# Holding one GpSimd cast behind a VectorE chain, and emitting half of an S1 sum two units sooner

## The chip, the cores and the metric

The kernel runs on one core of a Trainium2 chip. The metric is device time in microseconds (us); each time below is a median of several executions, but for two runs of one execution each. Positions such as "at 67.10" are us from the start of a profiled span. The span is about 1.8 us shorter than the measured time. The experiments were made in two sessions on two chips, and each is compared with the kernel before of its own session: 263.33 us for e2, e3, e5 and e6, 263.17 us for e7, e8, e10 and e11.

## The reference, cut to what matters

```python
q_s = softmax(q, over d);  k_s = softmax(k, over s)         # 8 batches, 8 heads, 576 x 64
kv  = einsum('bhsd,bhse->bhde', k_s, v)
x   = einsum('bhsd,bhde->bhse', q_s, kv)  -> reshaped to 4608 x 512
h   = x @ w_in                             # 512 -> 2048
out = (h * sigmoid(h)) @ w_out             # 2048 -> 512, float32
```

## The kernel before

The 4608 tokens go in nine chunks of 512. Apart from the start (chunk 0 and half of the first product of chunk 1), both matrix products of a chunk are done with seven block products in place of eight. This needs sums and differences of blocks, which VectorE makes: `S1` to `S4` for the second product. TensorE's program is a list of units of work; `plan(u, f)` emits `f` just ahead of unit `u`. An "h add" is VectorE adding a product, from the PSUM banks where matmuls write, to a sum `h`; it frees these banks for later matmuls. Each engine runs what was emitted for it in order and waits on semaphores where data demand it.

```python
def s_op(t, i, f0=0, f1=HF):                     # on VectorE, both inputs in SBUF
    in0, in1, op = {
        1: (blk(t, 0, 1), blk(t, 1, 1), ALU.add),
        2: (SS[1], blk(t, 0, 0), ALU.subtract),
        3: (blk(t, 0, 0), blk(t, 0, 1), ALU.subtract),
        4: (blk(t, 1, 0), SS[2], ALU.subtract),
    }[i]
    ...
def full(t):                                      # chunks 2 to 6
    ...
    for i, x in ((1, 4), (2, 5), (3, 15), (4, 19)):
        plan(u + x, lambda i=i: s_op(t - 1, i))
    for i in range(2):                            # the attention of the next batch, b = t + 1
        plan(u + (3, 10)[i], lambda i=i: exp_q(b, i))              # ScalarE
        plan(u + (7, 11)[i], lambda i=i: qsum(b, i))               # VectorE: zq, then rzq = 1/zq
        plan(u + (16, 17)[i], lambda i=i: qnorm(b, i, nc.gpsimd))  # GpSimd: eq * rzq
        plan(u + (2, 11)[i], lambda i=i: vcast(b, i, nc.gpsimd))   # GpSimd: v to bf16
    ...
last = NCH - 1
plan(begin[NCH] - 9, lambda: s_op(last, 1, 4, 8))  # half of the last chunk's S1
```

The softmax here doesn't subtract the row's maximum and nothing guards it: scores larger than these inputs give would overflow.

Of the kernel before, what the change touches and what calls it, by code (L numbers as in the profile page):

```python
# [17 lines left out]
def kernel(  # L18
# [9 lines left out]
    nc = tc.nc  # L28
# [12 lines left out]
    NCH = NT // TCH  # L41
# [21 lines left out]
    SS = {i: glob.tile([128, HF, HT], FP16, name=f"S{i}") for i in (1, 2, 4)}  # L63
# [8 lines left out]
    gate = glob.tile([1, 1], FP32, name="gate")  # L72
# [14 lines left out]
    def copy(eng, o, i):  # L87
        if eng is nc.scalar:
            eng.copy(out=o, in_=i)  # L89
        else:  # L90
            eng.tensor_copy(o, i)  # L91

    def load(b, name, src, cc, eng):
        t = ld.tile([128, 2, J * D], FP32, name=name)
        st[b][name, cc] = t
        x = src[b].rearrange("(g r) (p j) d -> g (r p) (j d)", r=2, j=J)
        eng.dma_start(out=t, in_=x.rearrange("g x y -> x g y")[:, 2 * cc:2 * cc + 2, :])

    def jgd(b, name, cc):
        return st[b][name, cc].rearrange("p g (j d) -> p j g d", d=D)  # L100
# [4 lines left out]
    def exp_q(b, cc, g0=0, g1=2):  # L105
        if "eq" not in st[b]:
            st[b]["eq"] = ap.tile([128, J, NG * D], BF16, name="eq")
        nc.scalar.activation(  # L108
            out=half(st[b]["eq"], cc)[:, :, g0:g1], in_=jgd(b, "qt", cc)[:, :, g0:g1], func=ACT.Exp
        )  # L110

    def exp_k(b, cc):
        nc.scalar.activation(out=half(ek, cc), in_=jgd(b, "kt", cc), func=ACT.Exp)  # L113

    def vcast(b, cc, eng, g0=0, g1=2):
        o = vaug[:, :, 2 * cc + g0:2 * cc + g1, 0:D]
        i = jgd(b, "vt", cc)[:, :, g0:g1, :]
        copy(eng, o, i)

    def qsum_pair(b, cc):  # L120
        e = half(st[b]["eq"], cc)
        t1 = mp.tile([128, 2 * TCH], FP32, name="h0", bufs=1)[:, 0:J * D]
        t1 = t1.rearrange("p (j g d) -> p j g d", g=2, d=D // 2)
        t2 = mp.tile([128, 2 * TCH], FP32, name=f"h{cc + 1}", bufs=1)[:, 0:J * D // 2]
        t2 = t2.rearrange("p (j g d) -> p j g d", g=2, d=D // 4)
        nc.gpsimd.tensor_tensor(  # L126
            out=t1, in0=e[:, :, :, 0:D // 2], in1=e[:, :, :, D // 2:D], op=ALU.add
        )
        nc.gpsimd.tensor_tensor(
            out=t2, in0=t1[:, :, :, 0:D // 4], in1=t1[:, :, :, D // 4:D // 2], op=ALU.add  # L130
        )
        st[b]["t2", cc] = t2
# [11 lines left out]
    def qsum(b, cc, gs=None):  # L144
        new_zq(b)
        z, e = st[b]["zq"][:, cc], half(st[b]["eq"], cc)
        if gs is None:
            nc.vector.reduce_sum(out=z, in_=e, axis=AX.X)  # L148
        else:
            nc.vector.reduce_sum(out=z[:, :, gs], in_=e[:, :, gs, :], axis=AX.X)  # L150
        if gs != 0:
            nc.vector.reciprocal(out=st[b]["rzq"][:, cc], in_=z)  # L152

    def qnorm(b, cc, eng):
        e = half(st[b]["eq"], cc)
        r = st[b]["rzq"][:, cc]
        eng.tensor_tensor(  # L157
            out=e, in0=e, in1=r[:, :, :, None].to_broadcast([128, J, 2, D]), op=ALU.mult
        )
# [6 lines left out]
    def q_transpose(b):  # L166
        nc.sync.dma_start_transpose(
            out=new_qt(b).rearrange("x j c y -> x (j c) y"),
            in_=st[b]["eq"].rearrange("x j c -> x (j c)"),
        )  # L170
# [38 lines left out]
    def kv_both(b):  # L209
        kv(b, 0)  # L210
        kv(b, 1)
        kvcopy(b)
# [137 lines left out]
    def group_silu(t, i, f, n):  # L350
        x = group_bank(t, False) if i is None else four(t, i)
        nc.scalar.activation(out=group_out(t, f, n), in_=x, func=ACT.Silu, scale=1.0 / XS)  # L352

    def group(t, g, i, on=None, defer=False):
        bank = 0 if i in (1, 6, 7, 4) else 6 if t == 1 else 2
        w, f0, f1 = WS[g], 4 * g + 8, 4 * g
        a, bb = {
            1: (wa(0, f0), xb(t, 0, 0)),
            2: (wa(1, f0), xb(t, 1, 0)),
            3: (w[3], xb(t, 1, 1)),  # L360
            4: (wa(1, f1), XS4[3]),
            5: (w[0], XS4[0]),
            6: (w[1], XS4[1]),
            7: (w[2], XS4[2]),
        }[i]
        for p in range(4):
            for c in range(2):
                nc.tensor.matmul(  # L368
                    out=PS[:, bank + p // 2, (p % 2) * HT:(p % 2) * HT + width(t)],
                    lhsT=a[:, c, p * 128:(p + 1) * 128],  # L370
                    rhs=bb[:, c, 0:width(t)],
                    start=(i in (1, 2, 5) and c == 0 and p % 2 == 0),
                    stop=(i in (2, 3, 4) and c == 1 and p % 2 == 1),
                    skip_group_check=True,
                )
        on = on or {}
        if i == 1:
            group_snap(t, 0)
        elif i == 2:
            group_add(t, 0)  # L380
        elif i == 6:
            group_snap(t, 1, on.get(1, nc.scalar))
        elif i == 7:
            group_snap(t, 2, on.get(2, nc.scalar))
            group_add(t, 2)
        elif i == 4:
            group_silu(t, None, f1, 0)
        elif i == 3:
            if not defer:
                group_silu(t, 2, f1, 1)  # L390
                group_silu(t, 0, f0, 0)
            group_add(t, 1)
# [37 lines left out]
    def blk(t, kh, th):  # L430
        return GTS[t % 2][:, kh * HF:(kh + 1) * HF, th * HT:(th + 1) * HT]

    def s_op(t, i, f0=0, f1=HF):
# [6 lines that stand above are left out]
        f = slice(f0, f1)  # L440
        o = blk(t, 0, 1) if i == 3 else SS[i]
        nc.vector.tensor_tensor(out=o[:, f], in0=in0[:, f], in1=in1[:, f], op=op)  # L442
# [170 lines left out]
    def plan(u, f):  # L613
        at.setdefault(u, []).append(f)
# [7 lines left out]
    begin = {1: len(units)}  # L622
# [3 lines left out]
    def b_units(t, order):  # L626
        got = []
        for i in order:
            got.append(lambda t=t, i=i: prod(t, i, 0))

            def second(t=t, i=i):
                prod(t, i, 1)
                after(t, i)

            got.append(second)
        return got
# [11 lines left out]
    def full(t):  # L648
        begin[t] = u = len(units)
        b = t + 1  # L650
        bs = b_units(t - 1, ORDER)
        gs = [
            lambda g=g, i=i: group(t, g, i, {1: nc.vector} if g else {2: nc.vector}, True)
            for g in (1, 0)
            for i in ORDER
        ]
        for x in 2 * four_pairs:
            units.append({"b": bs, "g": gs}[x].pop(0))
        for i, x in ((1, 4), (2, 5), (3, 15), (4, 19)):
            plan(u + x, lambda i=i: s_op(t - 1, i))  # L660
        for g, at3 in ((1, (13, 17, 15)), (0, (23, 28, 25))):
            f1, f0 = 4 * g, 4 * g + 8
            for i, x, f, n in zip(range(3), at3, (f0, f0, f1), (0, 1, 1)):
                plan(u + x, lambda i=i, f=f, n=n: group_silu(t, i, f, n))
        more = b + 1 < B
        for i in range(2):
            plan(u + (3, 10)[i], lambda i=i: exp_q(b, i))
            plan(u + (7, 11)[i], lambda i=i: qsum(b, i))
            plan(u + (16, 17)[i], lambda i=i: qnorm(b, i, nc.gpsimd))
            plan(u + (2, 11)[i], lambda i=i: vcast(b, i, nc.gpsimd))  # L670
            plan(u + (6, 4)[i], lambda i=i: exp_k(b, i))
            if more:
                plan(u + (5, 12)[i], lambda i=i: load(b + 1, "qt", q, i, nc.sync))
                plan(u + (8, 6)[i], lambda i=i: load(b + 1, "kt", k, i, nc.sync))
                plan(u + (22, 23)[i], lambda i=i: load(b + 1, "vt", v, i, nc.sync))
        plan(u + 17, lambda: q_transpose(b))
        plan(u + 15, lambda: kv_both(b))
        plan(u + 22, lambda: xt(t + 1, 0, nc.vector))
        plan(u + 27, lambda: xt(t + 1, 1))
        plan(u, lambda: (xs_op(t, 1), xs_op(t, 2), xs_op(t, 3), xs_op(t, 4)))  # L680
# [24 lines left out]

    begin[NCH] = len(units)
    last = NCH - 1
    plan(begin[NCH] - 9, lambda: s_op(last, 1, 4, 8))
    plan(begin[NCH] - 7, lambda: s_op(last, 2, 4, 8))
    plan(begin[NCH], lambda: (s_op(last, 1, 0, 4), s_op(last, 2, 0, 4), s_op(last, 3)))  # L710
    plan(begin[NCH] + 6, lambda: s_op(last, 4))
# [139 lines left out]
```

## Time and profile before

| | before |
|---|---|
| median of 4 executions (of the first 3, which the prediction had: 263.27) | 263.32 us (263.2 to 263.8) |
| span of the profiled one | 261.6 us |
| TensorE busy | 252.6 us, 97% |
| chunk 2: S1 on VectorE | 1.90 us (67.10 to 69.00) |
| chunk 2: second v cast on GpSimd | 66.76 to 67.93 |

In a timeline line the columns are start, duration, engine, source line, operation, output<-input, shapes, and in brackets the idle time before it with what ended it. VectorE is DVE, ScalarE is ACT, GpSimd is POOL, TensorE is PE. To judge a wait of TensorE here, use starts: undisturbed bursts of eight matmuls start 0.87 us apart. What exceeds that is lateness.

This answer for S1's source line, in the kernel before, gives count, shortest, median and longest duration in ns:

```profile
L442 DVE TENSOR_TENSOR S<-GT x9: 681/1215/1897, 67.1 to 245.2; 128x2048 f16<-128x2048 f16 x7, 128x1024 f16<-128x1024 f16 x2
```

The median is 1215 ns and one instance took 1897: the one in chunk 2.

### The profile page before, as it was taken

To read this page: it belongs to the slowest core of one execution; us is meant where nothing else is said; L and a number is where in the kernel's file an instruction comes from. 1 tells how busy PE (TensorE), PEld (TensorE's weight loads), DVE (VectorE), ACT (ScalarE), POOL (GpSimd) and SP (SyncE) were. 2 spreads that over 40 slices of the span, in tenths; PEclk is the share of its full clock that TensorE was granted. 3 is DMA by queue.
4 is the path that set the end of the run, shared out by engine and by line. 5 is a ranking of instruction groups with operands and counts; after the bars stand their busy time and mean duration, and the time that the engine had idled before them with its cause. 6 is when DMAs were issued, how large, how long until landed. Compare 5 with 4: busy or idle time off the path is not lost.

```text
span 261.6 us, 6410 instructions
## 1 busy us (share of the span) xinstructions
PE 252.6 (97%) x2732; PEld 203.2 (78%) x2732; DVE 207.7 (79%) x268; ACT 187.6 (72%) x212; POOL 65.7 (25%) x62
## 2 busy tenths in 40 slices
PE   8799999999999999999999999999999999999992
PEld 3457655656887888888888888888888888888881
DVE  2867797888997999799979997999798548855832
ACT  5766887898994799579957995799573748484610
POOL 1743791651160306030603060306000000000003
PEclk9999999999999999999999999999999999999999
DMA  7999999689979486957794869640534003300624
GB/s 244 335 192 297 299 319 333 259 184 391 307 278 238 111 220 230 205 142 189 262 230 118 218 233 167 180 89 3 90 76 87 3 0 78 85 3 1 139 64 120
DMA packets 35452, 45.89 MB, mean 175 GB/s; under 512 B 16208, under 2 KB 19984, under 8 KB 35424
## 3 DMA queue, kind: packets, MB, share of 16 engines
q1 hardware_dynamic: 29568, 33.69, 47.4%
q0 software_dynamic: 5616, 11.60, 17.0%
q8 instruction: 21, 0.34, 0.5%
q10 hardware_dynamic: 240, 0.20, 0.2%
q14 instruction: 7, 0.06, 0.1%
HBM read 36.70 MB, written 9.44 MB: 176 GB/s over the span
## 4 chain that ended last, share of the span: by engine, by line
PE 79%; DVE 6%; DMA 5%; issue 4%; POOL 3%; ACT 1%; POOLq 0%; DVEq 0%; ACTq 0%
PE PS L468 34%; PE PS L368 33%; PE PS L405 5%; DMA qt<-in_q_dram 5%; PE PS L276 2%; PE PS L228 2%; PE PS L189 2%; DVE h L346 1%; POOL W L545 1%; DVE S L442 1%; DVE GT L442 1%; DVE zq L148 1%; POOL out_dram L730 1%; POOL h L126 0%; DVE h L91 0%
## 5 line engine op out<-in xcount | busy, mean ns | idle before, releaser
L346 DVE TENSOR_TENSOR h<-PS,h 128x1024 f32<-128x1024 f32 (+1 forms) x45 | 54.0, 1199 | 13.0 <-ACT h L89 6.8
L468 PEld LDWEIGHTS <-GT 128*128 128x128 f16 x512 | 49.6, 98 | 6.8 <-issue 1.0
L368 PEld LDWEIGHTS <-WS 128*128 128x128 f16 x480 | 46.8, 98 | 7.2 <-issue 1.1
L468 PE MATMUL PS<-W,GT 128*128 128x256 f16 x384 | 49.1, 273 | 0.0
L368 PE MATMUL PS<-XS,WS 128*128 128x256 f16 (+1 forms) x360 | 46.3, 272 | 0.5 <-DVE h L346 0.5
L352 ACT ACTIVATE GT<-h 128x1024 f16<-128x1024 f32 (+1 forms) x45 | 46.1, 1047 | 0.3 <-DVE h L346 0.3
L89 ACT COPY h<-PS 128x1024 f32<-128x1024 f32 (+1 forms) x35 | 35.1, 1004 | 13.6 <-PE PS L368 13.1
L157 POOL TENSOR_TENSOR eq<-eq,rzq 128x1152 bf16<-128x1152 bf16 x13 | 27.8, 2135 | 58.2 <-DVE rzq L152 56.5
L468 PEld LDWEIGHTS <-S 128*128 128x128 f16 x384 | 37.1, 98 | 5.5 <-issue 1.0
L368 PEld LDWEIGHTS <-W 128*128 128x128 f16 x360 | 34.7, 98 | 4.8 <-issue 0.5
L468 PE MATMUL PS<-T,S 128*128 128x256 f16 x256 | 32.7, 273 | 0.0
L368 PE MATMUL PS<-XT,W 128*128 128x256 f16 (+1 forms) x240 | 29.5, 272 | 0.1
L352 ACT ACTIVATE GT<-PS 128x1024 f16<-128x1024 f32 (+1 forms) x15 | 15.3, 1017 | 18.9 <-PE PS L368 18.9
L91 POOL CAST vaug<-vt 128x1152 bf16<-128x1152 f32 x12 | 14.9, 1242 | 43.7 <-DMA vt<-in_v_dram 34.9
L108 ACT ACTIVATE eq<-qt 128x1152 bf16<-128x1152 f32 (+1 forms) x18 | 19.1, 1059 | 2.7 <-DMA qt<-in_q_dram 2.7
L730 POOL DMA_DIRECT2D out_dram<-ow x5 | 2.7, 546 | 72.5 <-DVE ow L715 72.5
L113 ACT ACTIVATE ek<-kt 128x1152 bf16<-128x1152 f32 x16 | 18.4, 1154 | 1.4 <-DMA kt<-in_k_dram 1.4
L148 DVE TENSOR_REDUCE zq<-eq 128x18 f32<-128x1152 bf16 x12 | 16.1, 1344 | 3.8 <-ACT eq L108 3.8
L258 PE MATMUL PS<-XT,W 128*128 128x288 f16 x128 | 16.6, 286 | 0.5 <-DVE XT L91 0.2
L468 PE MATMUL PS<-W,S 128*128 128x256 f16 x128 | 16.5, 273 | 0.0
L488 DVE SCALAR_TENSOR_TENSOR ow<-PS,sc 128x512 f32<-128x512 f32 x7 | 4.8, 691 | 14.4 <-ACT sc L484 14.4
L258 PEld LDWEIGHTS <-W 128*128 128x128 f16 x128 | 12.3, 97 | 4.9 <-issue 1.6
(78 smaller groups left out, 346.3 us busy)
## 6 DMA issues: line engine op xcount, KB each, us to landing
out_dram<-ow SPq DMA_DIRECT2D x64, 128.0 KB, 2.4
qt<-in_q_dram SPq DMA_DIRECT2D x12, 576.0 KB, 4.6
kt<-in_k_dram SPq DMA_DIRECT2D x12, 576.0 KB, 5.4
vt<-in_v_dram SPq DMA_DIRECT2D x12, 576.0 KB, 5.4
qt<-in_q_dram POOLq DMA_DIRECT2D x4, 576.0 KB, 10.6
kt<-in_k_dram POOLq DMA_DIRECT2D x4, 576.0 KB, 13.3
vt<-in_v_dram POOLq DMA_DIRECT2D x4, 576.0 KB, 12.7
W<-in_moe_w_out_dram POOLq DMA_DIRECT2D x4, 512.0 KB, 14.9
```

The costliest lines, as they stand in the source:

```text
L89: eng.copy(out=o, in_=i)
L91: eng.tensor_copy(o, i)
L108: nc.scalar.activation(out=half(st[b]["eq"], cc)[:, :, g0:g1], in_=jgd(b, "qt", cc)[:, :, g0:g1], func=ACT.Exp)
L113: nc.scalar.activation(out=half(ek, cc), in_=jgd(b, "kt", cc), func=ACT.Exp)
L148: nc.vector.reduce_sum(out=z, in_=e, axis=AX.X)
L157: eng.tensor_tensor(out=e, in0=e, in1=r[:, :, :, None].to_broadcast([128, J, 2, D]), op=ALU.mult)
L258: nc.tensor.matmul(out=PS[:, 2 * (fb % 3) + n, 0:S // 2], lhsT=W1[:, c, fb * 128:(fb + 1) * 128], rhs=XTS[0][:, c, n * (S // 2):(n + 1) * ...
L346: nc.vector.tensor_tensor(out=four(t, i), in0=group_bank(t, True), in1=four(t, i), op=ALU.add)
L352: nc.scalar.activation(out=group_out(t, f, n), in_=x, func=ACT.Silu, scale=1.0 / XS)
L368: nc.tensor.matmul(out=PS[:, bank + p // 2, (p % 2) * HT:(p % 2) * HT + width(t)], lhsT=a[:, c, p * 128:(p + 1) * 128], rhs=bb[:, c, 0:wid ...
L405: nc.tensor.matmul(out=PS[:, 2 + tb, :], lhsT=GTS[t % 2][:, fc, tb * 128:(tb + 1) * 128], rhs=W2[:, fc, :], start=(fc == 0), stop=(fc == N ...
L468: nc.tensor.matmul(out=PS[:, bank, m * HN:(m + 1) * HN], lhsT=a[:, fc, m * 128:(m + 1) * 128], rhs=bb[:, fc, :], start=(first and fc == 0) ...
```

## The change

The intent is to keep the second v cast of chunk 2 off GpSimd until S2 is done, so that it does not run beside S1. A 1x1 copy on GpSimd reads one element of S2, and the cast stands behind it in order. The second part emits half of the last chunk's S1 two units sooner.

```diff
+    def vcast_at(t, b, cc):
+
+        if t == 2 and cc == 1:
+            nc.gpsimd.tensor_copy(gate, SS[2][0:1, 0, 0:1])
+        vcast(b, cc, nc.gpsimd)
...
-            plan(u + (2, 11)[i], lambda i=i: vcast(b, i, nc.gpsimd))
+            plan(u + (2, 6 if t == 2 else 11)[i], lambda i=i: vcast_at(t, b, i))
...
-    plan(begin[NCH] - 9, lambda: s_op(last, 1, 4, 8))
+    plan(begin[NCH] - 11, lambda: s_op(last, 1, 4, 8))
```

## The prediction

> **What bounds the kernel now.** I read three views, from coarse to fine: the page's busy times, the chain of waits cut to chunk 2 (56 to 90 us from the span's start), and the timelines of VectorE, GpSimd and TensorE over the same stretch. The page says who is scarce:
>
> ```profile
> PE 252.6 (97%) x2732; PEld 203.2 (78%) x2732; DVE 207.7 (79%) x268; ACT 187.6 (72%) x212; POOL 65.7 (25%) x62
> ```
>
> TensorE is busy 97% of the span at a granted clock of 0.999. Work taken off another engine buys nothing, unless TensorE stands still waiting for that engine. So the question is only where it stands still. The chain that ended last, in chunk 2, answers it:
>
> ```profile
> 65.05 0.89 PE PS L368 x8
> 65.94 0.02 issue
> 65.96 1.22 DVE h L91
> 67.18 1.82 DVE S L442
> 69.01 0.02 issue
> 69.03 1.23 DVE S L442
> 70.26 1.27 DVE zq L148
> ...
> 75.12 1.08 DVE h L346
> 76.20 2.61 DVE GT L442
> ...
> 79.35 1.23 DVE h L346
> 80.57 0.04 issue
> 80.61 1.03 PE PS L368 x8
> ```
>
> For 14.6 us (65.96 to 80.57) the chain leaves TensorE and lies on VectorE without a break; after 80.61 it is TensorE again until about 253 us, where the closing copies and stores begin. So VectorE sets the end of the kernel only here. Two of its links are long: S1 (1.82 us) and S3 (the GT line, 2.61). The timeline of VectorE, then of GpSimd, shows why:
>
> ```profile
> 67.10 1.90 DVE L442 TENSOR_TENSOR S<-GT 128x2048 f16<-128x2048 f16 x1
> 69.03 1.23 DVE L442 TENSOR_TENSOR S<-S,GT 128x2048 f16<-128x2048 f16 x1
> 76.11 2.70 DVE L442 TENSOR_TENSOR GT<-GT 128x2048 f16<-128x2048 f16 x1
> ```
>
> ```profile
> 66.76 1.16 POOL L91 CAST vaug<-vt 128x1152 bf16<-128x1152 f32 x1 [1.29 <-DMA vt<-in_v_dram]
> 72.03 2.12 POOL L157 TENSOR_TENSOR eq<-eq,rzq 128x1152 bf16<-128x1152 bf16 x1 [4.10 <-DVE rzq L152]
> 75.61 2.12 POOL L157 TENSOR_TENSOR eq<-eq,rzq 128x1152 bf16<-128x1152 bf16 x1 [1.47 <-ACT GT L352]
> ```
>
> S1 starts while the second v cast runs (66.76 to 67.92) and takes 1.90 us; in chunk 3, with no GpSimd work beside it, the same S1 takes 1.22 (94.21 to 95.43). S1 ends at 69.00, 1.08 us after the cast. S3 ends at 78.81, again 1.08 us after the second q normalization (77.73); chunk 3's S3 ends at 104.89 against 103.81, 1.08 once more. So VectorE does next to nothing while the GpSimd instruction lasts and then needs 1.08 us. S1 lost 1.90 - 1.22 = 0.68 us to the cast.
>
> The cost on TensorE is smaller than the chain looks:
>
> ```profile
> 69.25 1.04 PE L468 MATMUL PS<-W,GT 128*128 128x256 f16 x8
> 70.31 1.05 PE L468 MATMUL PS<-T,S 128*128 128x256 f16 x8
> ...
> 79.10 1.04 PE L468 MATMUL PS<-W,GT 128*128 128x256 f16 x8
> 80.61 1.03 PE L368 MATMUL PS<-XS,WS 128*128 128x256 f16 x8 [0.48 <-DVE h L346]
> ```
>
> Undisturbed bursts of eight matmuls start 0.87 us apart. At 70.31 the burst that needs S2 is 70.31 - 69.25 - 0.87 = 0.19 us late; at 80.61 the burst whose PSUM banks the h add frees is 80.61 - 79.10 - 0.87 = 0.64 late. Together 0.83 us: no speeding up of VectorE in chunk 2 can gain more.
>
> **What the Trainium skill says.** "SBUF — State Buffer", section "Who interferes with whom": a VectorE instruction with two SBUF inputs contends with a GpSimd instruction that reads SBUF; the loser blocks until the other is through; one with at most one SBUF input, outside the two-port modes, does not contend; a reduction on trn2 never does. The trace agrees on each: S1 and S3 (two SBUF inputs) end 1.08 us after the GpSimd instruction. The zq reduction at 73.48, half of it beside a q normalization, takes 1.34 us, against 1.35 at 70.17 with GpSimd idle. The h adds (one input in PSUM) take 1.16 us beside a normalization and up to 1.23 alone. "VectorE: DVE Perf Modes", section "Side-by-side: where the cycles go for N=2048 bf16", gives about 1224 ns for 2048 elements at two per cycle; the undisturbed S operations here take 1.22 us, so 1.22 is what S1 should return to. "Perfetto Trace Analysis", section "GPSIMD Engine Instruction", calls a GpSimd span in a profile unreliable. Here the casts repeat within 1.16 to 1.17 us and the VectorE ends follow at the same 1.08 us, so I use the ends.
>
> **The change, part by part.** In the built programs, every engine's order of instructions can be compared.
>
> The S1 half: it is emitted two units sooner, but no other VectorE instruction is emitted in those two units. VectorE's order and the waits of that instruction are the same in both programs. In the profile it starts at 235.06, as soon as the h add in front of it ends, and VectorE idles 2.95 us later before 238.69. **Worth: 0.00 us.**
>
> The held cast: GpSimd gets one instruction more, a 1x1 copy from S2 into a one-element tile, which waits for S2; the cast stands behind it. Its earlier place (unit 6 instead of 11) changes no order on GpSimd. Chunk 3's S2 gets a wait for that copy, some 25 us after it. I work the new times out from the old ones:
> - S1 67.10 to 68.32 (1.22 instead of 1.90); S2 68.35 to 69.57. **0.68 us sooner.**
> - S2's matmuls: TensorE is ready at 69.25 + 0.87 = 70.12, S2 is done: the 0.19 us go.
> - GpSimd: the 1x1 copy costs 0.18 us (the other gate copy, at 8.46). With a release of some 0.14 us (rzq to the normalization: 71.89 to 72.03) the cast runs about 69.9 to 71.1. Beside it stands the zq reduction, which does not contend. The kv matmuls need the cast at 75.73: over 4 us of slack.
> - The rest of the VectorE chain moves 0.68 sooner. The earliest it could run: the h add at 71.81 waits for a ScalarE copy that ends at 70.46 (new start 71.13); the second zq for an exp ending at 71.53 (new 72.80); the h add at 75.04 for matmuls ending near 74.06 (new 74.36). None bites.
> - The second normalization waits for rzq, done at 75.12, new 74.44. In chunk 2 it starts 0.49 us after rzq, in chunks 3 to 6 0.14 after; I see no cause for the difference in the records. If it stays, it runs 74.93 to 77.05, and S3 ends 1.08 later, at 78.13: 0.68 sooner. If it goes, S3 ends another 0.35 sooner.
> - The h add then ends at 79.89 instead of 80.57; TensorE would have been ready at 79.97 - 0.19 = 79.78, so it starts near 79.93: **0.68 us sooner**, 0.15 of the stall left. If the extra 0.35 goes too, the gain is capped at 0.83.
>
> After that the chain is TensorE's, burst behind burst, to the end, so the gain should arrive whole. Sum: 263.27 - 0.68 - 0.00 = 262.59, **262.6 us**, a quarter of a per cent.
>
> **The rivals.**
> 1. *The cast finds another victim.* Moved behind S2 it could block what follows. For it: GpSimd has to read the same 128x1152 f32 tile somewhere. Against: beside it are now a reduction and, at its very end, a 128x18 reciprocal, and a reduction shows no loss above. If I am wrong by a whole cast, the chain gives back up to 0.7: about 263.2.
> 2. *S3 swallows the gain.* S3 cannot end before the second normalization plus 1.08. If that normalization does not move with rzq (the profile names a ScalarE line as its releaser, ending at 75.30), it stays at 75.61 to 77.73, and S3 at 78.81. Then only the 0.19 at 70.31 can change, and it returns as waiting at 80.61: 263.3, no gain. Against: the wait it carries for ScalarE is for the exp that ended at 71.53, so rzq is the true releaser.
> 3. *The start of the normalization mends itself*, with another instruction in GpSimd's stream: 0.83 gained, 262.4.
> 4. *A later wait takes over*, a load or the transposed q of chunk 2. The transpose is issued when the normalization ends, so it moves with it; I see none that would bind.
>
> **Range and chances.** The core case and rival 3 make 262.4 to 262.6 and hold some three quarters of the weight; rivals 1, 2 and 4 make 262.9 to 263.3. The three runs before spread from 263.2 to 263.8, so 0.1 of noise goes on top. Range 262.3 to 263.1. Two per cent would be 5.3 us, six times the whole stall: faster 0.01, same 0.98, slower 0.01.
>
> **What would show each step right or wrong.** Right: chunk 2's S1 at 1.22 us; the second cast starting just after S2 at about 69.9; the zq reduction beside it still 1.34 to 1.35; S3 ending 1.08 us after the second normalization, both about 0.68 sooner; TensorE's wait at 80.61 shrunk from 0.48 to under 0.2; the last chunk's S1 half in the same place between the same neighbours. Wrong: a zq reduction or h add that grew; a normalization still starting at 75.61; a new TensorE gap after chunk 2 that gives the 0.68 back; or any gain traced to the last chunk.

## The result

The kernel after took 262.16 us (262.06 to 262.53, 4 executions), against 263.32 before: 1.16 us by the medians. The ratio is 0.9955, with a 95% interval of 0.9938 to 0.9972. A ratio is the mean time of one kernel's fast runs over that of the other's of the same rounds, so it is not quite the ratio of the medians. The time lies below the range of 262.3 to 263.1, and the gain is 1.7 times the 0.68 predicted. Against the threshold of 2% it counts as the same.

The lines below are the kernel after's. All lines after the inserted ones stand six higher than before, so L448 is the old L442. First the page's busy times, then the chain of waits in chunk 2 (start, us, what):

```profile
PE 251.4 (97%) x2732; PEld 203.0 (78%) x2732; DVE 206.8 (79%) x268; ACT 187.6 (72%) x212; POOL 66.3 (25%) x63
```

```profile
66.35 0.87 PE PS L374 x8
67.22 0.87 PE PS L474 x8
68.10 0.87 PE PS L374 x8
68.97 1.75 PE PS L474 x16
...
78.55 0.87 PE PS L474 x8
79.42 0.87 PE PS L374 x8
```

The 14.6 us on VectorE are gone from the chain: chunk 2 is TensorE's alone. VectorE, GpSimd and TensorE in that stretch:

```profile
66.66 1.22 DVE L448 TENSOR_TENSOR S<-GT 128x2048 f16<-128x2048 f16 x1
67.90 1.22 DVE L448 TENSOR_TENSOR S<-S,GT 128x2048 f16<-128x2048 f16 x1
69.05 1.34 DVE L154 TENSOR_REDUCE zq<-eq 128x18 f32<-128x1152 bf16 x1
73.73 0.27 DVE L158 RECIPROCAL rzq<-zq 128x18 f32<-128x18 f32 x1
74.99 2.35 DVE L448 TENSOR_TENSOR GT<-GT 128x2048 f16<-128x2048 f16 x1
```

```profile
69.19 0.18 POOL L123 CAST gate<-S 1x1 f32<-1x1 f16 x1 [3.57 <-DMA out_dram<-ow]
69.32 1.15 POOL L91 CAST vaug<-vt 128x1152 bf16<-128x1152 f32 x1
70.90 2.12 POOL L163 TENSOR_TENSOR eq<-eq,rzq 128x1152 bf16<-128x1152 bf16 x1 [0.43 <-issue]
74.14 2.12 POOL L163 TENSOR_TENSOR eq<-eq,rzq 128x1152 bf16<-128x1152 bf16 x1 [1.12 <-DVE rzq L158]
```

```profile
68.81 1.04 PE L474 MATMUL PS<-W,GT 128*128 128x256 f16 x8
69.68 1.04 PE L474 MATMUL PS<-T,S 128*128 128x256 f16 x8
...
78.38 1.04 PE L474 MATMUL PS<-W,GT 128*128 128x256 f16 x8
79.26 1.04 PE L374 MATMUL PS<-XS,WS 128*128 128x256 f16 x8
```

S1 is back at 1.22 us. The copy starts 0.07 us after S2 ends (the label in brackets names a DMA; for the same program in e2_hold_only it names S2's line), and the cast runs beside the zq reduction, which keeps its 1.34 us. Two things were not as predicted. The second normalization starts at 74.14, only 0.14 us after rzq is done (74.00), where the kernel before needed 0.49. And TensorE has no lateness left at all: 69.68 - 68.81 and 79.26 - 78.38 are both an undisturbed 0.87 or 0.88.

Laid beside each other, the two traces split the difference in three. As a marker I take the burst of nine transposes in chunk 1, which ends the opening (the stretch that still hangs on the first loads). From the marker to the burst behind the h add is the stretch where the change acts; from there to the last matmul is the rest.

| profiled run | marker at | marker to h-add burst | h-add burst to last matmul |
|---|---|---|---|
| before | 34.80 | 45.82 | 175.67 |
| after | 34.34 | 44.91 | 175.68 |
| difference | 0.46 | 0.91 | -0.01 |

So 0.91 us came from chunk 2, more than the 0.68 predicted and more than my cap of 0.83. The last chunk gave nothing. Another 0.46 us stood in the opening, which the change does not touch. The experiments ask what each of these is.

### The profile page after: what moved, and what is told of

Read it like the earlier page. It is cut to its first block, busy times and chain, and to the rows that moved or that the text cites. A ratio compares the mean times of both kernels' runs of the same rounds, so it can differ in the third digit from the quotient of the medians.

```text
span 260.3 us, 6411 instructions
## 1 busy us (share of the span) xinstructions
PE 251.4 (97%) x2732; PEld 203.0 (78%) x2732; DVE 206.8 (79%) x268; ACT 187.6 (72%) x212; POOL 66.3 (25%) x63
## 4 chain that ended last, share of the span: by engine, by line
PE 88%; DVE 4%; ACT 2%; POOL 2%; DMA 1%; issue 1%; POOLq 0%; ACTq 0%
PE PS L474 37%; PE PS L374 35%; PE PS L411 5%; PE PS L264 3%; PE PS L282 2%; PE PS L234 2%; PE PS L195 2%; DMA qt<-in_q_dram 1%; DVE eq L163 1%; DVE zq L154 1%; ACT sg L256 1%; POOL out_dram L736 1%; ACT eq L108 1%; DVE GT L257 1%; POOL h L132 0%
```

## The experiments

All were correct. The table gives, for each profiled run, the marker, S1 and S2 on VectorE, the delay from the end of rzq to the start of each normalization on GpSimd, and TensorE's lateness in chunk 2 (at S2's burst, at group 3's, which is the burst at 73.02 in the kernel before, and behind the h add; start differences minus 0.873 per burst, taken from the nanoseconds of the traces, so that sums of the rounded lines can be off by 0.01 or 0.02).

| run | marker | S1 | S2 | delay of 1st / 2nd normalization | lateness | sum |
|---|---|---|---|---|---|---|
| before | 34.80 | 1.90 | 1.23 | 0.14 / 0.49 | 0.19 + 0.08 + 0.64 | 0.91 |
| e3_s1_only | 34.30 | 2.10 | 1.23 | 0.14 / 0.49 | 0.40 + 0.07 + 0.64 | 1.11 |
| after | 34.34 | 1.22 | 1.22 | 0.13 / 0.14 | 0 | 0 |
| e2_hold_only | 34.90 | 1.22 | 1.23 | 0.14 / 0.14 | 0 | 0 |
| e5_copy_no_hold | 34.16 | 1.22 | 2.06 | 0.13 / 0.14 | 0.34 + 0.08 + 0.29 | 0.71 |
| e6_gate_s1 | 34.47 | 1.22 | 1.23 | 0.13 / 0.14 | 0 | 0 |
| e7_two_copies | 34.44 | 1.22 | 1.23 | 0.50 / 0.15 | 0 | 0 |
| e10_three_copies | 34.60 | 1.22 | 1.23 | 0.15 / 0.14 | 0 | 0 |
| e11_early_copy | 34.78 | 2.19 | 1.22 | 0.14 / 0.14 | 0.49 + 0.08 + 0.29 | 0.85 |
| e8_cast_twice | 34.32 | 2.07 | 2.06 | 0.14 / 0.14 | 1.20 + 0.08 + 0.29 | 1.57 |

From the h-add burst to the last matmul, all ten traces have 175.67 or 175.68 us. Nothing that happens in chunk 2 or before is given back later. The marker does not catch all of the opening: e10_three_copies has 45.11 us from the marker to the h-add burst, where the other runs without lateness have 44.91, and lost these 0.20 us in chunk 1, before 41.1.

### The S1 move alone (e3_s1_only)

```diff
--- before
-    plan(begin[NCH] - 9, lambda: s_op(last, 1, 4, 8))
+    plan(begin[NCH] - 11, lambda: s_op(last, 1, 4, 8))
```

> The kernel before with only the S1 half emitted two units sooner. Compared instruction by instruction, the built program is the same as that of the kernel before, order, waits and semaphore counts, so this run is also a second look at the kernel before. Theory A (the move is empty): within 0.1 us of the kernel before in the same rounds, the last chunk's S1 half still right behind the h add and 2.9 us of VectorE idling after it. Theory B (the move is worth something in the last chunk, part of the 1.16 us): 0.2 us or more faster. It also asks whether the opening is fixed by the program: the profile before reached TensorE's chunk 2 (the burst at 65.05) 0.45 us later than the profile after did. Theory C (chance of the first loads): this profile's opening may fall anywhere between or beyond the two. Theory D (bound to the program): it repeats 65.05 within 0.1. The second q normalization of chunk 2 started 0.49 us after rzq in the profile before and 0.10 in the profile after: if that is bound to the program it is 0.49 here again; if it was a chance of one execution it is about 0.1 to 0.14.

Measured: 263.29 us (5 executions) against 263.33 before (9), ratio 0.9997 (0.9984 to 1.0009). The move is empty, as the identical program says. The lines of this run, VectorE, GpSimd and TensorE:

```profile
66.62 2.10 DVE L442 TENSOR_TENSOR S<-GT 128x2048 f16<-128x2048 f16 x1
74.58 0.27 DVE L152 RECIPROCAL rzq<-zq 128x18 f32<-128x18 f32 x1
```

```profile
66.49 1.16 POOL L91 CAST vaug<-vt 128x1152 bf16<-128x1152 f32 x1 [1.47 <-DMA vt<-in_v_dram]
75.33 2.12 POOL L157 TENSOR_TENSOR eq<-eq,rzq 128x1152 bf16<-128x1152 bf16 x1 [1.47 <-DVE rzq L152]
```

```profile
68.77 1.04 PE L468 MATMUL PS<-W,GT 128*128 128x256 f16 x8
70.03 1.05 PE L468 MATMUL PS<-T,S 128*128 128x256 f16 x8 [0.23 <-DVE S L442]
...
80.33 0.92 PE L368 MATMUL PS<-XS,WS 128*128 128x256 f16 x7 [0.48 <-DVE h L346]
```

As a second look at the kernel before, it says more. The marker is at 34.30, not 34.80, with the same program: the opening varies from execution to execution (theory C). The cast came 0.13 us before S1 instead of 0.34, so S1 lost 2.10 - 1.22 = 0.88 us instead of 0.68, and TensorE's lateness is 1.11 instead of 0.91. And the delay of 0.49 us before the second normalization is there again (74.84 to 75.33), so it is not a chance of one execution. The profile here names rzq as its releaser, where the first profile named a ScalarE line: that label was not to be relied on.

### The held cast alone (e2_hold_only)

```diff
--- after
-    plan(begin[NCH] - 11, lambda: s_op(last, 1, 4, 8))
+    plan(begin[NCH] - 9, lambda: s_op(last, 1, 4, 8))
```

> The kernel after without the S1 move: only the cast is held. Its built program is that of the kernel after, instruction by instruction. Theory A: all of the gain is the held cast: 0.9 us (the chunk 2 part: TensorE's lateness of 0.18 at S2's burst, 0.08 at group 3's and 0.64 at the burst behind the h add) plus whatever the opening gives; so 0.9 us faster than the kernel before when many runs are averaged, 1.1 or more if the opening's 0.45 comes with the program. Theory B: the S1 move carried part, and this is 0.2 us or more slower than the kernel after's 1.16 us gain for that reason. Chunk 2 should again show no TensorE wait, S1 at 1.22 us and the normalization about 0.1 us after rzq.

Measured: 262.45 us (262.12 to 262.93, 5 executions) against 263.33 in the same rounds, 0.88 us by the medians, ratio 0.9967 (0.9954 to 0.9979). The program is that of the kernel after, and the gain 0.88 instead of 1.16. Its marker is at 34.90, later than in either first profile, and the stretch from there to the h-add burst is 44.91, as in the kernel after. So the cast's part of the change, which is the hold and the copy that makes it, is the whole gain, and the opening does not come with the program. The nine executions of this program together have a median of 262.27.

### The copy without the hold (e5_copy_no_hold)

```diff
--- after
-            nc.gpsimd.tensor_copy(gate, SS[2][0:1, 0, 0:1])
+            nc.gpsimd.tensor_copy(gate, ident[0:1, 0:1])
```

> The kernel after with the 1x1 copy reading a tile that is ready from the start instead of S2: one GpSimd instruction more than before, but the cast is not held. Theory A (the lock is what cost): S1 is again about 1.9 us, ending about 1.08 us after the cast, and the time is that of the kernel before, 0 to 0.35 us faster. For the normalization that started 0.49 us after rzq: theory E (position in GpSimd's instruction stream: one instruction more shifts it) makes it 0.10 to 0.14 here, and the kernel some 0.3 us faster than before; theory F (coincidence in time with what else runs then) leaves it at about 0.49 and the time at that of the kernel before.

Measured: 262.67 us (4 executions), against 263.33, ratio 0.9976 (0.9961 to 0.9992): more than the 0 to 0.35 expected. The lines of GpSimd and of VectorE:

```profile
66.52 2.19 POOL L91 CAST vaug<-vt 128x1152 bf16<-128x1152 f32 x1 [1.29 <-DMA vt<-in_v_dram]
```

```profile
66.47 1.22 DVE L448 TENSOR_TENSOR S<-GT 128x2048 f16<-128x2048 f16 x1
67.72 2.06 DVE L448 TENSOR_TENSOR S<-S,GT 128x2048 f16<-128x2048 f16 x1
```

S1 started at 66.47, 0.05 us ahead of the cast, and took its 1.22 us. The cast waited for it and its span grew to 2.19 us, to 68.71. Then S2 was stretched, ending at 69.78, 1.07 us behind the cast. My expectation named S1 as the victim; it was S2. The collision costs S2 0.83 us, where it cost S1 0.68 and 0.88 in the two looks at the kernel before. But the lateness behind the h add fell from 0.64 to 0.29: the normalization's delay has shrunk by 0.35 with nothing but one more GpSimd instruction. The sum of lateness fell by 0.20 or 0.40 against the two looks at the kernel before. The rest of the profiled execution's gain goes with its early marker (34.16). The other three executions have no trace, so what their part of the median comes from is not shown, and 0.66 is no clean measure of the copy.

### The gate on S1 instead of S2 (e6_gate_s1)

```diff
--- after
-            nc.gpsimd.tensor_copy(gate, SS[2][0:1, 0, 0:1])
+            nc.gpsimd.tensor_copy(gate, SS[1][0:1, 0, 0:1])
```

> The kernel after with the 1x1 copy reading S1 instead of S2, so that the cast is free as soon as S1 is done, while S2 runs. Theory G (an exclusive lock, held by whoever starts first): S2 starts 0.03 us after S1, ahead of the copy, so the copy itself is blocked until S2 is through (its span about 1.1 us instead of 0.18, or its start that much later), the cast starts where it does in the kernel after, S2 stays at 1.22 us, and the time is that of the kernel after within 0.15 us. Theory H (GpSimd takes the ports from a running VectorE instruction): S2 is stretched by about 0.7 to 1.2 us, and the gain over the kernel before shrinks to 0.3 us or less.

Measured: 262.31 us (4 executions) against 263.33, ratio 0.9964 (0.9951 to 0.9978). GpSimd and VectorE:

```profile
68.06 1.24 POOL L123 CAST gate<-S 1x1 f32<-1x1 f16 x1 [2.87 <-DVE S L448]
69.24 1.15 POOL L91 CAST vaug<-vt 128x1152 bf16<-128x1152 f32 x1
```

```profile
68.03 1.23 DVE L448 TENSOR_TENSOR S<-S,GT 128x2048 f16<-128x2048 f16 x1
```

Theory G holds. S2 had started 0.03 us earlier and kept its 1.23 us. The copy of a single element took 1.24 us instead of 0.18, because it could only finish after S2, and the cast started 1.21 us after S2 did, against 1.42 in the kernel after.

### Two and three added instructions (e7_two_copies, e10_three_copies)

```diff
--- after
             nc.gpsimd.tensor_copy(gate, SS[2][0:1, 0, 0:1])
+            nc.gpsimd.tensor_copy(gate, ident[0:1, 0:1])      # e10: this line twice
```

> The kernel after with a second 1x1 copy (of a tile that is ready) behind the one that reads S2: two GpSimd instructions more than the kernel before. The start that was 0.49 us after rzq belonged to the 68th place of GpSimd's program (counting from zero, as built), where the second normalization stands in the kernel before. Theory E (the delay belongs to that place of the stream): now the first normalization stands there, and it starts about 0.45 to 0.5 us after its rzq, while the second starts 0.14 after its own; the time stays within 0.2 us of the kernel after. Theory E2 (any added GpSimd instruction heals it, the place does not matter): both start 0.14 us after.

> The kernel after with two more 1x1 copies of a ready tile: three GpSimd instructions more than before. Theory E: the 68th place is now the wait in front of the first normalization, which waits anyway, so the delay shows nowhere: both normalizations start 0.14 us after their rzq. Theory E2 says the same here; together with the two-copy run this tells them apart. The cast starts about 0.2 us later than in the kernel after, at no cost.

Measured, one execution each: 262.23 and 262.56 us, beside 263.17 for the kernel before. With two added instructions, VectorE and GpSimd show:

```profile
70.60 0.27 DVE L159 RECIPROCAL rzq<-zq 128x18 f32<-128x18 f32 x1
73.83 0.27 DVE L159 RECIPROCAL rzq<-zq 128x18 f32<-128x18 f32 x1
```

```profile
71.37 2.12 POOL L164 TENSOR_TENSOR eq<-eq,rzq 128x1152 bf16<-128x1152 bf16 x1 [0.56 <-ACT eq L108]
74.25 2.12 POOL L164 TENSOR_TENSOR eq<-eq,rzq 128x1152 bf16<-128x1152 bf16 x1 [0.76 <-DVE rzq L159]
```

Now the first normalization starts 0.50 us after its rzq (70.87 to 71.37) and the second 0.15 after its own. The delay moved to the other instruction, which now has the 68th place of GpSimd's program. With three added, that place belongs to a wait that waits anyway, and the delay is nowhere (0.15 and 0.14); the cast came 0.47 us later behind S2 than in the kernel after, where I had expected 0.2, at no cost. So the delay belongs to a place in the stream (theory E); these two programs were run once each, and the next run tests the same from the other side. A delayed first normalization costs TensorE nothing, since no S operation runs beside it (lateness 0 in the table).

### One early copy, nothing held (e11_early_copy)

```diff
--- before
+    plan(b1 + 10, lambda: nc.gpsimd.tensor_copy(gate, ident[0:1, 0:1]))
     plan(b1 + 10, lambda: exp_q(2, 0))
```

> The kernel before with nothing but one 1x1 copy on GpSimd added, in chunk 1, some 20 us ahead of chunk 2, where GpSimd idles. The cast is not held. Theory E (place in the stream): the second normalization of chunk 2 starts 0.14 us after rzq, S3 ends 0.35 us sooner relative to it, TensorE's lateness behind the h add falls from 0.64 to about 0.29, and the kernel is 0.35 us (0.3 to 0.45) faster than the kernel before, with S1 or S2 still stretched by the cast. Theory F (a coincidence in time within chunk 2): 0.49 again and no gain.

Measured: 262.93 us (262.62 to 263.36, 5 executions) against 263.17, ratio 0.9990 (0.9976 to 1.0003): 0.24 us by the medians where I had expected 0.3 to 0.45, and too small a gain to call. The profile is clear: the second normalization starts 0.14 us after rzq, and the lateness behind the h add is 0.29, although the copy is some 20 us away. VectorE's second rzq, the second normalization, and the bursts around the h add (the last one cut off by the view):

```profile
75.13 0.27 DVE L152 RECIPROCAL rzq<-zq 128x18 f32<-128x18 f32 x1
75.54 2.12 POOL L157 TENSOR_TENSOR eq<-eq,rzq 128x1152 bf16<-128x1152 bf16 x1 [1.12 <-DVE rzq L152]
79.38 1.04 PE L468 MATMUL PS<-W,GT 128*128 128x256 f16 x8
80.54 0.71 PE L368 MATMUL PS<-XS,WS 128*128 128x256 f16 x5
```

In the profiled execution the load of v landed later, so the cast covered S1 almost whole:

```profile
67.08 2.19 DVE L442 TENSOR_TENSOR S<-GT 128x2048 f16<-128x2048 f16 x1
```

That cost 0.97 us at S1 and took back most of the 0.35. It was also the slowest of the five.

### The cost doubled (e8_cast_twice)

```diff
--- after
-            nc.gpsimd.tensor_copy(gate, SS[2][0:1, 0, 0:1])
+            vcast(b, cc, nc.gpsimd)
         vcast(b, cc, nc.gpsimd)
```

> Not held, and the second v cast of chunk 2 is done twice in a row in place of cast and copy: the suspected cost doubled, with the same number of GpSimd instructions as the kernel after. Theory A (a GpSimd instruction that follows another at once keeps the ports, VectorE waits for both): S1 or S2 is stretched by about 1.16 us more than in the run with the copy that does not hold, and the time is about 1.1 us above that run's 262.67, near 263.7 to 263.9. Theory B (a waiting VectorE instruction gets in between the two casts, the second cast then waits and runs beside the reduction): S1 and S2 together lose no more than with one cast, and the time stays near 262.7.

Measured: 263.65 us (4 executions) against 263.17, ratio 1.0014 (0.9999 to 1.0028). That is 0.48 us slower than the kernel before, where the run with copy and no hold was 0.66 faster, each in its own rounds: about 1.1 us apart. VectorE, then the second of the two casts:

```profile
66.63 2.07 DVE L448 TENSOR_TENSOR S<-GT 128x2048 f16<-128x2048 f16 x1
68.74 2.06 DVE L448 TENSOR_TENSOR S<-S,GT 128x2048 f16<-128x2048 f16 x1
```

```profile
67.69 2.03 POOL L91 CAST vaug<-vt 128x1152 bf16<-128x1152 f32 x1
```

Neither theory is right as it stood. The first cast ran to 67.63, then S1 got in, as theory B said: it ended at 68.70 while the second cast waited (span 2.03 instead of 1.16). But then the second cast went ahead of S2, which had started after it, so S2 lost 0.84 us on top of S1's 0.85. The time is nearly theory A's (263.65 against 263.7 to 263.9), by another way; the lateness in chunk 2 grew from 0.71 to 1.57, by 0.86 where theory A had 1.1. In this trace the waiting instructions of the two sides take turns in the order of their starts.

## Why the prediction was wrong

**What held.** The S1 move is worth nothing: same program, 263.29 against 263.33. The mechanism of the cast is right in both directions. S1 went from 1.90 to 1.22 us, the reduction beside the cast kept 1.34, the 0.19 us at S2's burst went, S3 ended 1.08 us after the second normalization in every profile, and the gain reached the end whole (175.67 and 175.68). Rivals 1, 2 and 4 did not happen: no other victim, the normalization moved with rzq, no later wait. One reading was too narrow: "the casts repeat within 1.16 to 1.17 us" leaves out the cast at 52.35 of the kernel before, in chunk 1, which took 2.15. It stood behind a VectorE operation with two SBUF inputs (`T`, L452, 51.63 to 53.48), which itself ended 1.08 us after the normalization before the cast. So that trace already showed both directions.

**The step that failed: "If it stays, it runs 74.93 to 77.05".** I had seen that the second normalization started 0.49 us after rzq in chunk 2 and 0.14 elsewhere, found no cause, and built the central case on its staying. It belongs to a place in GpSimd's program, and the change, by adding one instruction, moves it off: 0.14 us in the kernel after, and 0.14 in e5_copy_no_hold and e11_early_copy, which add an instruction and hold nothing. Rival 3 was the true case and I gave it too little weight. S3 then ended 1.03 us sooner relative to S1's start (77.34 - 66.66 against 78.81 - 67.10), where I had 0.68. On TensorE the step is worth 0.15 us: I had left 0.15 of the stall behind the h add standing, and none was left.

**The cap of 0.83 was too low.** I counted two late bursts. There is a third, in the kernel before at 73.02, 0.08 us late. These are its TensorE lines:

```profile
72.07 1.04 PE L468 MATMUL PS<-T,S 128*128 128x256 f16 x8
73.02 1.03 PE L368 MATMUL PS<-XT,WS 128*128 128x256 f16 x8
```

Group 3's matmuls wait, in the built program, for the h add that started at 71.81, and start 0.05 us after it ends (72.97). The sum is 0.91 and all of it went: my 0.68, the 0.15 of the step that failed, and the 0.08 of this burst.

**The 0.68 was one execution's number.** The loss is the part of the cast that still runs when S1 starts, less 0.14 us: 67.93 - 67.10 - 0.14 = 0.69 in the first profile, 67.65 - 66.62 - 0.14 = 0.89 in e3_s1_only, 68.21 - 67.08 - 0.14 = 0.99 in e11_early_copy, where 0.68, 0.88 and 0.97 were lost. The cast starts when a load has landed, so the loss varies. Over the two looks at the kernel before, chunk 2 had 0.91 and 1.11 us to give.

**The range was too narrow.** I allowed 0.1 us for noise. The marker alone lies between 34.16 and 34.90 in ten traces, and between 34.30 and 34.80, or 34.34 and 34.90, for one and the same program. In the first two profiles it happened to favour the kernel after by 0.46 us. This is luck and no part of the change: 263.27 - 0.91 = 262.36 would have lain in the range, and what took the measured 262.16 below it is, as far as the traces show, the landing of v and the opening, which vary from execution to execution. Over nine executions each program's median says 262.27 for the change, and 263.33 for the kernel before in the rounds of e3_s1_only and e2_hold_only: 1.06 us.

How the 0.91 to 1.11 us of chunk 2 divide: taking away only the delay leaves a sum of lateness of 0.71 or 0.85 (e5_copy_no_hold, e11_early_copy), so the hold itself is worth those 0.71 to 0.85, and at the burst behind the h add the added instruction alone is worth 0.64 - 0.29 = 0.35. The two overlap with the chance of the landing, so they do not add up to a tenth.

**Open.** What delays GpSimd by 0.35 us at that place, the traces do not show: no transfer of instructions is recorded at that moment. The transfers of instructions that they do record nearby begin after the delay has ended: on queue q14 each of the ten traces has one between 73.80 and 77.25, with the delay or without it, and in the three traces that have the delay it begins 1.0 to 3.8 us after the late start. So a wait for instructions is neither shown nor ruled out. Only that the delay goes with the place is shown. No version beyond the kernel after was tried: its chunk 2 has no lateness left, so nothing here points to one.

## What to carry to other kernels

When VectorE is on the critical path, look for GpSimd instructions that read SBUF beside VectorE instructions with two SBUF inputs, and order them with a one-element copy where the held instruction has slack; the cast had over 4 us here. Compare the built programs before believing that an earlier emission moves anything: an instruction with the same neighbours is the same program. And when one instance of a repeated pair starts late for no visible reason, do not assume that it stays: an added instruction can remove it, and a second profile of the unchanged kernel tells chance from program.

## What the Trainium skill lacked or had wrong

- "SBUF — State Buffer", section "Who interferes with whom", is confirmed in both directions: S1 at 1.90 to 2.19 us behind the cast, the cast at 2.19 behind S1. It says that issue order and not the shape of the operation decides who blocks; the runs add the extreme case, a 1x1 copy that took 1.24 us instead of 0.18 beside S2.
- The same section says that the second instruction fully blocks, which the runs bear out but for a small start: VectorE's S operations need 1.07 to 1.08 us after GpSimd's instruction is through, some 0.14 less than their 1.22 alone. The section has no such figure. It also lacks who is next when both sides keep coming: two casts and S1, S2 took turns, 2.07 and 2.06 us.
- No page has this delay that goes with a place in GpSimd's instruction stream: 0.35 us on one instruction, in the same place in three profiles (0.49, 0.49, 0.50 us after rzq instead of 0.14). Should it prove to be a wait for instructions, which no run shows, it would belong to "Runtime: NRT & Kernel Launch", section "Instruction fetch mechanics".
- "Perfetto Trace Analysis", section "GPSIMD Engine Instruction", calls GpSimd spans unreliable. For these casts and normalizations the ends were good to 0.01 us: S3 followed the normalization's end by 1.08 us in all ten profiles, and S1 or S2 the end of a cast by 1.07 in the five that collided.
